# Folding the layer norm's scale of the first two row tiles into the exponential, moving the Q weights ahead of the fourth x tile, and writing a new order of the first stage

## The chip, the cores and the metric

One NeuronCore of a Trainium2 chip runs the whole program. The metric is the device time of one execution in microseconds (us). Before the change four runs gave a median of 213.01 us (212.72 to 213.26). The profile is one further execution of the same program; its own device time is 213.03 us, and the span from its first to its last instruction is 211.4 us.

## The reference

Shapes: x is 2048 rows of 512, `wqkv` 512x1536, `wo` 512x512, `w_gate` and `w_up` 512x1792, `w_down` 1792x512, all bf16. Attention has 32 heads of 16.

```python
xn = (x - mean(x)) / sqrt(var(x) + 1e-5)               # row by row
q, k, v = xn @ wqkv                                     # 32 heads of 16
phi = lambda t: where(t > 0, t + 1, exp(t)) + 1e-6
kv  = einsum("bhsd,bhse->bhde", phi(k), v);  z = sum over rows of phi(k)
o   = (phi(q) @ kv) / (phi(q) . z + 1e-6)
out = x + o @ wo + (silu(xn @ w_gate) * (xn @ w_up)) @ w_down
```

## The kernel before

**Engines.** Every operation is put into one list by `K.add` with the keys that it reads and writes (lines 40 to 67). Each engine runs its own operations strictly in the order of that list, and semaphore waits are made from the keys. TensorE (PE) does matmuls and transposes, VectorE (DVE) and ScalarE (ACT) read PSUM, GpSimd (POOL) works in SBUF only, and SyncE (SP) and ACT issue DMAs. A DMA that waits for its data holds up everything behind it on the engine that issues it.

**Stage 1** takes the 2048 rows in 16 tiles of 128. The order in which its steps stand in the list is written out by hand as a string of letters with a tile number (lines 352 to 361). The letters, by engine:

- DVE: `S` statistics of a row tile (L228 and L231); `L` normalise (L241); `V` a PSUM copy; `s` and `u` the last step of phi for k and for q (L316).
- ACT: `R` rstd = exp(-0.5 ln(var + eps)) (L235 and L237); `A` normalise with two per-row operands (L251); `E` a PSUM copy of a transposed tile (L276); `x` and `y` the exponential for k and q (L305).
- POOL: `N` the product mean*rstd that `A` needs (L246); `P` normalise (L256 and L259); `m` and `n` the clamp min(exp, 1 + 1e-6) (L309).
- PE: `T` four 128x128 transposes (L269); `k` and `q` a projection of one tile, four 128x512 matmuls (L297); `G` four matmuls that add xn^T phi(k) to four PSUM banks (L321); `F` filler matmuls.
- SP: `D`, a DMA transpose of a normalised tile into `xnT` (L284).

So phi is a chain over three engines: PE projection, ACT exp, POOL min, DVE max-and-add, which leaves `pk` or `pq` in SBUF. Projections take PSUM banks 4 to 7 in turn (`nextbank`), so a projection can't start until `s` or `u` has read the one four before it. Tiles 0 to 2 are transposed by PE (banks 0 to 2, copied out by ACT or DVE), tiles 3 to 15 by DMA. Instead of v and kv the kernel forms G = xn^T phi(k) (512x512, banks 0 to 3) and multiplies it by the V weights later.

Ahead of all that stand the table load, the loads (lines 185 to 196: x tile 0 in two halves, then x1, the K weights in two halves, x2, and the Q weights in two halves with x3 between them on SP's queue), some constants on POOL, and `NWARM` = 10 matmuls of 512 columns on constants (L218).

**Stage 2** starts with the loads of the other weights, issued by SP behind the last `D`. It runs 56 gate and up steps (`gu`, L384, in four chunks of 512 rows, Silu on ACT L392, product on DVE L397), the small matmuls that turn G into M = blockmask(kv) @ wo (L409, L457), the sum z of phi(k) (`z_add`: ten tiles on POOL, six on DVE), the division of phi(q) by its denominator (`pz_mul` on POOL, `divide` on DVE, a DMA transpose), and 16 output tiles (`ogroup`, L463 and L467) with the residual added by DVE (L473).

Of the kernel before, what the change touches and what calls it, by code (L numbers as in the profile page):

```python
# [9 lines left out]
P = 128  # L10
# [13 lines left out]
NWARM = 10  # L24
NFILL = 3
# [82 lines left out]
def bass_parallel_sum__linear_attn_block__swiglu_ffn__prompt_kernel(nc, A_x, A_wqkv, A_wo, B_x, B_w_gate, B_w_up, B_w_down, out):  # L108
# [5 lines left out]
    with contextlib.ExitStack() as es:  # L114
# [6 lines left out]
        xn = sb("xn", [P, NT, D], bf)  # L121
        xnT = sb("xnT", [P, NDC, S], bf)
# [28 lines left out]
        nm = sb("nm", [P, NT], f32)  # L151
        banks = [E(nc.psum_tensor("pb%d" % i, [P, 512], f32)) for i in range(8)]

        def B(i):
            return ("bank", i)
# [30 lines left out]
        for h, eng in ((0, "sp"), (1, "act")):  # L186
            load(eng, ("x", 0, h), x_sb[:, 0, h * 256:h * 256 + 256], xin[0:P, h * 256:h * 256 + 256])
        xload("sp", 1)
        wload("act", 1, 0, 2)
        wload("sp", 1, 1, 2)  # L190
        xload("act", 2)
        wload("act", 0, 0, 2)
        xload("sp", 3)
        wload("sp", 0, 1, 2)
        for t in range(4, 16):
            xload("sp", t)
# [27 lines left out]
        def xk(t):  # L224
            return [("x", t)] if t else [("x", 0, 0), ("x", 0, 1)]
# [7 lines left out]
        def rs(t):  # L233
            sl = slice(t, t + 1)
            K.add("act", lambda e: e.activation(lnv[:, sl], mv[:, t, 1:2], ACT.Ln, bias=eps5[:, :], scale=1.0),  # L235
                  r=[("mv", t), ("eps5",)], w=[("lnv", t)])
            K.add("act", lambda e: e.activation(rstd[:, sl], lnv[:, sl], ACT.Exp, scale=-0.5),  # L237
                  r=[("lnv", t)], w=[("rs", t)])

# [27 lines left out]
        def transp(t, b, lo=0, hi=NDC):  # L267
            tb = tview(b, hi - lo)
            K.add("pe", [(lambda e, c=c: e.transpose(tb[:, c - lo, :], xn[:, t, c * P:(c + 1) * P], ident[:, :]))  # L269
                         for c in range(lo, hi)], r=[("xn", t), ("ident",)], w=[B(b)])  # L270

        def evac(t, b, eng="act", lo=0, hi=NDC):
            src = tview(b, hi - lo)
            dst = xnT[:, lo:hi, t * P:(t + 1) * P]
            if eng == "act":
                K.add("act", lambda e: e.activation(dst, src, ACT.Copy), r=[B(b)], w=[("xnT", t, lo)])  # L276
            else:
                K.add("dve", lambda e: e.tensor_copy(dst, src), r=[B(b)], w=[("xnT", t, lo)])

        def xkeys(t):  # L280
            return [("xnT", t, 0), ("xnT", t, 2)] if t == 0 else [("xnT", t, 0)]

        def dmat(t):
            K.add("sp", lambda e: e.dma_start_transpose(out=xnT[:, :, t * P:(t + 1) * P], in_=xn[:, t, :]),  # L284
                  r=[("xn", t)], w=[("xnT", t, 0)], dma=True)
# [9 lines left out]
        def proj(col, i, t):  # L295
            b = nextbank()
            K.add("pe", [(lambda e, c=c: e.matmul(  # L297
                banks[b][:, :], xnT[:, c, t * P:(t + 1) * P], wqkv[:, c, col:col + D],
                start=(c == 0), stop=(c == NDC - 1))) for c in range(NDC)],
                r=xkeys(t) + [("wqkv", i, 0), ("wqkv", i, 1)], w=[B(b)])  # L300
            at[i, t] = b

        def phi_exp(i, t):
            b = at[i, t]
            K.add("act", lambda e: e.activation(ef[:, b - 4, :], banks[b][:, :], ACT.Exp), r=[B(b)], w=[("ef", b - 4)])  # L305

        def phi_min(i, t):
            buf, bkey = ef[:, at[i, t] - 4, :], ("ef", at[i, t] - 4)
            K.add("pool", lambda e: e.tensor_scalar(  # L309
                out=buf, in0=buf, scalar1=1.0 + 1e-6, scalar2=0.0, op0=ALU.min, op1=ALU.max),  # L310
                r=[bkey], w=[bkey])

        def phi_sum(i, t):
            b = at[i, t]
            dst, dkey = ((pk[:, t, :], ("pk", t)) if i else (pq[:, t, :], ("pq", t)))
            K.add("dve", lambda e: e.scalar_tensor_tensor(  # L316
                out=dst, in0=banks[b][:, :], scalar=1e-6, in1=ef[:, b - 4, :], op0=ALU.max, op1=ALU.add),
                r=[B(b), ("ef", b - 4)], w=[dkey])

        def gacc(t):  # L320
            K.add("pe", [(lambda e, c=c: e.matmul(  # L321
                banks[c][:, :], xn[:, t, c * P:(c + 1) * P], pk[:, t, :],
                start=(t == 0), stop=(t == NT - 1))) for c in range(NDC)],
                r=[("xn", t), ("pk", t)], w=[B(c) for c in range(NDC)])
# [4 lines left out]
        def z_add(half, i):  # L329
            acc, key = zacc[:, half, :], ("zacc", half)  # L330
            t = NZP * half + i
            first, fkey = (pk[:, t - 1, :], ("pk", t - 1)) if i == 1 else (acc, key)
            K.add("dve" if half else "pool",
                  lambda e: e.tensor_tensor(out=acc, in0=first, in1=pk[:, t, :], op=ALU.add),  # L334
                  r=[fkey, ("pk", t)], w=[key])

        def stat(t):
# [4 lines left out]
            "S": stat, "R": rs, "L": lna_dve, "P": lna_pool, "N": nmr, "A": lna_act, "T": lambda t: transp(t, t % 4),  # L342
            "E": lambda t: evac(t, t % 4), "V": lambda t: evac(t, t % 4, "dve"), "D": dmat,
            "k": lambda t: proj(D, 1, t), "x": lambda t: phi_exp(1, t), "m": lambda t: phi_min(1, t), "s": lambda t: phi_sum(1, t),
            "q": lambda t: proj(0, 0, t), "y": lambda t: phi_exp(0, t), "n": lambda t: phi_min(0, t), "u": lambda t: phi_sum(0, t), "G": gacc,
            "F": lambda t: keep_busy(t, 256)}

        def run(text):
# [4 lines left out]
            S0 R0 S1 L0 R1 L1 S2 T0 E0 F2 T1 V1 R2 L2 k0 k1 x0 m0 S3 T2 S4 x1 m1 E2 R4 s0 q1 R3 L4 k2 x2 N3 A3  # L353
            q2 s1 m2 y1 S5 R5 G0 D4 S6 s2 n1 G1 q0 y2 G2 D3 u1 R6 q4 N5 A5 S8 y0 k3 n2 N6 A6 u2 k4 y4 x3 n0 x4
            n4 m3 u0 m4 S13 D5 q3 R8 u4 s3 P8 D6 S7 k5 y3 R13 D8 n3 G3 s4 x5 k6 R7 S9 R9 N7 q6 G4 m5 A7 u3 s5
            S12 x6 q5 G5 N9 m6 S10 A9 y6 s6 y5 q8 R10 D7 k8 N13 n6 R12 u6 y8 G6 n5 x8 D9 u5 A13 k7 x7 S15 S11 k9
            P10 n8 u8 x9 R11 m8 D10 s8 m7 q9 m9 R15 P15 s7 y9 q7 G7 k10 D13 n9 L11 L12 s9 y7 q10 D11 G8 y10 n7
            n10 S14 G9 R14 x10 u7 u9 u10 k11 m10 N14 x11 s10 D15 q13 y13 A14 D12 m11 n13 s11 q11 y11 k12 D14 u13
            x12 m12 k13 k15 n11 x15 m15 u11 G10 x13 m13 s12 G11 q15 q14 y15 n15 s13 s15 k14 x14 m14 y14 q12 s14
            G12 y12 n12 n14 u15 G13 G14 u14 u12 G15  # L360
# [34 lines left out]
        def hop(j):  # L395
            C, fc = j // NFC, j % NFC
            K.add("dve", lambda e: e.tensor_tensor(  # L397
                out=hT[:, C % 2, fc, :], in0=banks[gb(j) + 1][:, :], in1=sil[:, j % 2, :], op=ALU.mult),
                r=[B(gb(j) + 1), ("sil", j % 2)], w=[("hT", C % 2, fc)])
# [37 lines left out]
        def divide(t):  # L437
# [3 lines left out]
                r=[("pz", i)], w=[("den", i)])  # L441
            K.add("dve", lambda e: e.tensor_scalar(
                out=den[:, i, :], in0=den[:, i, :], scalar1=1e-6, scalar2=None, op0=ALU.add),
                r=[("den", i)], w=[("den", i)])
# [121 lines left out]
```

## Time and profile before

| | |
|---|---|
| median of 4 runs | 213.01 us (212.72 to 213.26) |
| the profiled execution: device time | 213.03 us |
| the profiled execution: span | 211.4 us |
| PE busy | 208.1 us, 98% of the span |
| DVE / ACT / POOL busy | 125.4 / 69.8 / 55.7 us |
| first matmul on data (a transpose of x tile 0) | starts at 5.21 us |
| first projection | starts at 6.30 us |
| first matmul of stage 2 (L384) | starts at 48.48 us in the chain |
| last matmul ends, last output lands | 209.37 us, 211.36 us |

How to read it: all times inside the trace count from the first instruction of the span. A 512-column matmul is shown as 379 ns long, but the next one starts 216 ns after it, since matmuls are pipelined; a projection or a `G` of four matmuls therefore takes 0.863 us of PE's time. The device time is 1.65 us longer than the span.

### The profile page before, as it was taken

What the parts mean: (1) busy time and instruction counts of PE and PEld (TensorE: products, weight loads), DVE (VectorE), ACT (ScalarE), POOL (GpSimd) and SP (SyncE); (2) the same over time, 40 slices, a digit from 0 to 9 for tenths busy, and PEclk for the clock granted to TensorE, in tenths of its full rate; (3) what the DMA queues carried; (4) which work ended last, traced back from release to release, by engine and by line L of the source; (5) the groups of instructions that cost most, each with busy time, mean ns of one, the idle gap of its engine ahead of it and who ended that gap; (6) DMA issues with size and microseconds to landing.
All of it is one profiled execution on the core that took longest, in us unless ns stands there. A gap on an engine that the chain in (4) does not pass through costs nothing.

```text
span 211.4 us, 2659 instructions
## 1 busy us (share of the span) xinstructions
PE 208.1 (98%) x991; PEld 95.7 (45%) x991; DVE 125.4 (59%) x217; ACT 69.8 (33%) x138; POOL 55.7 (26%) x81
## 2 busy tenths in 40 slices
PE   7999999999999999999999999999999999999996
PEld 2444444444544444444444444444444444444455
DVE  3899985546874888564654765473649453532121
ACT  4697974546364332122131313121123122130000
POOL 3267664559913222220210220120204000000000
PEclk9999999999999999999999999999999999999999
DMA  6942333499910021103101011101011101100101
GB/s 183 357 115 49 72 63 62 119 380 372 353 43 0 8 45 25 50 0 53 25 25 45 4 29 50 25 25 50 19 34 25 50 16 38 25 25 9 40 25 53
DMA packets 26765, 15.78 MB, mean 75 GB/s; under 512 B 16512, under 2 KB 26752, under 8 KB 26752
## 3 DMA queue, kind: packets, MB, share of 16 engines
q1 hardware_dynamic: 25920, 14.88, 25.2%
q10 hardware_dynamic: 832, 0.72, 1.1%
q8 instruction: 8, 0.13, 0.3%
q14 instruction: 5, 0.04, 0.1%
HBM read 9.70 MB, written 2.10 MB: 56 GB/s over the span
## 4 chain that ended last, share of the span: by engine, by line
PE 96%; DVE 1%; DMA 1%; ACT 0%; issue 0%
PE pb L384 46%; PE pb L467 23%; PE pb L297 13%; PE pb L463 7%; PE pb L321 7%; DMA x_sb<-in_A_x_dram 1%; DVE stats L228 1%; PE pb L409 0%; PE pb L457 0%; PE pb L269 0%; DVE out_sb L473 0%; DVE xn L241 0%; DVE mv L231 0%; ACT lnv L235 0%; PE pb L425 0%; ACT rstd L237 0%
## 5 line engine op out<-in xcount | busy, mean ns | idle before, releaser
L392 ACT ACTIVATE sil<-pb 128x512 bf16<-128x512 f32 x56 | 33.3, 597 | 101.2 <-PE pb L384 98.8
L397 DVE TENSOR_TENSOR hT<-pb,sil 128x512 bf16<-128x512 f32 x56 | 38.0, 687 | 36.2 <-PE pb L384 33.4
L384 PE MATMUL pb<-xnT,wu 128*128 128x512 bf16 x224 | 57.8, 379 | 0.0
L384 PE MATMUL pb<-xnT,wg 128*128 128x512 bf16 x224 | 57.8, 379 | 0.0
L467 PE MATMUL pb<-wd,hT 128*128 128x512 bf16 (+1 forms) x238 | 51.2, 366 | 0.0
L434 POOL TENSOR_TENSOR pz<-pq,zbc 128x512 f32<-128x512 bf16 x16 | 18.5, 1162 | 86.0 <-DVE den L439 78.5
L467 PEld LDWEIGHTS pb<-wd,hT 128*128 128x128 bf16 x238 | 23.3, 98 | 25.1
L384 PEld LDWEIGHTS pb<-xnT,wu 128*128 128x128 bf16 x224 | 21.9, 98 | 26.0
L384 PEld LDWEIGHTS pb<-xnT,wg 128*128 128x128 bf16 x224 | 21.9, 98 | 25.9
L473 DVE TENSOR_TENSOR out_sb<-pb,x_sb 128x512 bf16<-128x512 f32 (+1 forms) x17 | 11.2, 661 | 33.5 <-PE pb L467 33.5
L297 PE MATMUL pb<-wqkv,xnT 128*128 128x512 bf16 x128 | 29.6, 379 | 0.0
L309 POOL TENSOR_SCALAR ef<-ef 128x512 bf16<-128x512 bf16 x32 | 19.5, 614 | 18.5 <-ACT ef L305 18.3
L305 ACT ACTIVATE ef<-pb 128x512 bf16<-128x512 f32 x32 | 18.3, 590 | 9.1 <-PE pb L297 8.8
L297 PEld LDWEIGHTS pb<-wqkv,xnT 128*128 128x128 bf16 x128 | 12.1, 98 | 15.4 <-ACT xnT L276 0.4
L446 DVE TENSOR_TENSOR pq<-pq,rden 128x512 bf16<-128x512 bf16 x16 | 17.5, 1092 | 0.6
L463 PE MATMUL pb<-M,pk 128*128 128x512 bf16 (+1 forms) x68 | 16.6, 366 | 0.0
L321 PE MATMUL pb<-pk,xn 128*128 128x512 bf16 x64 | 15.4, 379 | 0.0
L316 DVE SCALAR_TENSOR_TENSOR pk<-pb,ef 128x512 bf16<-128x512 f32 x16 | 10.8, 679 | 4.9 <-POOL ef L309 4.9
L228 DVE BATCH_NORM_STATS2 stats<-x_sb 128x6 f32<-128x512 bf16 x16 | 10.9, 680 | 3.3 <-DMA x_sb<-in_A_x_dram 3.2
L316 DVE SCALAR_TENSOR_TENSOR pq<-pb,ef 128x512 bf16<-128x512 f32 x16 | 10.7, 682 | 3.6 <-POOL ef L309 3.5
L439 DVE TENSOR_REDUCE den<-pz 128x32 f32<-128x512 f32 x16 | 10.8, 675 | 0.0
L334 POOL TENSOR_TENSOR zacc<-zacc,pk 128x512 f32<-128x512 f32 x8 | 10.3, 1292 | 0.6
(46 smaller groups left out, 76.9 us busy)
## 6 DMA issues: line engine op xcount, KB each, us to landing
out_dram<-out_sb SPq DMA_DIRECT2D x15, 128.0 KB, 1.7
x_sb<-in_A_x_dram SPq DMA_DIRECT2D x14, 128.0 KB, 5.0
wg<-in_B_w_gate_dram SPq DMA_DIRECT2D x2, 896.0 KB, 7.7
wu<-in_B_w_up_dram SPq DMA_DIRECT2D x2, 896.0 KB, 10.0
wd<-in_B_w_down_dram SPq DMA_DIRECT2D x2, 896.0 KB, 14.2
wqkv<-in_A_wqkv_dram ACTq DMA_DIRECT2D x2, 256.0 KB, 4.6
wqkv<-in_A_wqkv_dram SPq DMA_DIRECT2D x2, 256.0 KB, 5.0
wqkv<-in_A_wqkv_dram SPq DMA_DIRECT2D x1, 512.0 KB, 7.8
```

What stands on the lines that cost most here:

```text
L297: K.add("pe", [(lambda e, c=c: e.matmul(banks[b][:, :], xnT[:, c, t * P:(t + 1) * P], wqkv[:, c, col:col + D], start=(c == 0), stop=(c == ...
L305: K.add("act", lambda e: e.activation(ef[:, b - 4, :], banks[b][:, :], ACT.Exp), r=[B(b)], w=[("ef", b - 4)])
L309: K.add("pool", lambda e: e.tensor_scalar(out=buf, in0=buf, scalar1=1.0 + 1e-6, scalar2=0.0, op0=ALU.min, op1=ALU.max), r=[bkey], w=[bkey])
L316: K.add("dve", lambda e: e.scalar_tensor_tensor(out=dst, in0=banks[b][:, :], scalar=1e-6, in1=ef[:, b - 4, :], op0=ALU.max, op1=ALU.add), ...
L321: K.add("pe", [(lambda e, c=c: e.matmul(banks[c][:, :], xn[:, t, c * P:(c + 1) * P], pk[:, t, :], start=(t == 0), stop=(t == NT - 1))) for ...
L384: fns.append(lambda e, c=c, b=b, w_=w_: e.matmul(banks[b][:, :], w_[:, c, fc * P:(fc + 1) * P], xnT[:, c, C * 512:(C + 1) * 512], start=(c ...
L392: K.add("act", lambda e: e.activation(sil[:, j % 2, :], banks[gb(j)][:, :], ACT.Silu), r=[B(gb(j))], w=[("sil", j % 2)])
L397: K.add("dve", lambda e: e.tensor_tensor(out=hT[:, C % 2, fc, :], in0=banks[gb(j) + 1][:, :], in1=sil[:, j % 2, :], op=ALU.mult), r=[B(gb( ...
L434: K.add("pool", lambda e: e.tensor_tensor(out=pz[:, t % 2, :], in0=pq[:, t, :], in1=zbc[:, :], op=ALU.mult), r=[("pq", t), ("zbc",)], w=[( ...
L446: K.add("dve", lambda e: e.tensor_tensor(out=heads(pq[:, t, :]), in0=heads(pq[:, t, :]), in1=rden[:, i, :][:, :, None].broadcast_to([P, NH ...
L463: fns = [(lambda e, g=g: e.matmul(banks[bank][:, 0:hi - lo], pk[:, t, g * P:(g + 1) * P], M[:, g, lo:hi], start=(g == 0), stop=False)) for ...
L467: fns = [(lambda e, fc=fc: e.matmul(banks[bank][:, 0:hi - lo], hT[:, C % 2, fc, jj * P:(jj + 1) * P], wd[:, fc, lo:hi], start=False, stop= ...
```

## The change

Parts, as they stand in the code:

1. **Tiles 0 and 1 are only centred** ahead of their projections. Their transposed copies (`xcT`) hold x - mean, so a projection gives std times the wanted value. The exponential puts that right with two per-row operands, `scale=rstd` and `bias=ln(std)`; its result is std*exp(t). The clamp and the floor are scaled as well (`cap` = std*(1 + 1e-6), `flo` = std*1e-6), so `pk` and `pq` of these two tiles are std*phi. In G the other factor is `xg` = (x - mean)*rstd^2; in the sum z the rows are multiplied by rstd; in the division `pq` scales numerator and denominator alike, and the 1e-6 becomes `flo`.
2. Tile 0 is centred, transposed (two 128x128 transposes each, banks 0 and 1) and copied out in two halves. For tile 1 the mean comes from ACT (`M`: a Copy with an accumulated sum), without waiting for the statistics. Normalised copies of tiles 0 and 1 are still made (`P0` on POOL, `L1` on DVE) and go to `xnT` by two more DMA transposes (`D0`, `D1`) for stage 2; 15 in all, where there were 13. Tile 2 is transposed by PE as before (`X`, `Y`).
3. **Loads**: the Q weights' first half moves from ACT's queue to SP's, ahead of x3; the second half moves from SP's queue, behind x3, to ACT's. The K weights and x0 to x2 keep their places.
4. A projection's four matmuls are two groups of two, and each waits for its own half of the weights (and, for tiles 0 and 1, of the transposed tile).
5. `NWARM` goes from 10 to 8, and the filler `F2` is gone.
6. **The order string is new.** It holds the same 32 projections and 16 `G` groups, but starts k0 k1 q1 q0 k2 q2 G1 G0 G2, has only four `G` among the next 26 projections, and ends with nine `G` in a row. Normalising is done by POOL for 8 tiles (3 before), by ACT for 5 (7) and by DVE for 2 and the centred ones (6).
7. Scratch copies of tiles 0 and 1 lie in parts of `hT` and `pz` that are used later.

The diff, cut to its core:

```diff
-NWARM = 10
-NFILL = 3
+CENTRED = (0, 1)
+NWARM = 8
...
+        xhalf("sp", 0, 0)
+        xhalf("act", 0, 1)
         xload("sp", 1)
-        wload("act", 1, 0, 2)
-        wload("sp", 1, 1, 2)
+        wpart("act", 1, 0)
+        wpart("sp", 1, 1)
         xload("act", 2)
-        wload("act", 0, 0, 2)
-        xload("sp", 3)
-        wload("sp", 0, 1, 2)
-        for t in range(4, 16):
+        wpart("sp", 0, 0)
+        wpart("act", 0, 1)
+        for t in range(3, 16):
             xload("sp", t)
...
+        def powers(t):
+            sl = slice(t, t + 1)
+            K.add("act", lambda e: e.activation(std[:, sl], lnv[:, sl], ACT.Exp, scale=0.5), r=[("lnv", t)], w=[("std", t)])
+            K.add("act", lambda e: e.activation(r2[:, sl], lnv[:, sl], ACT.Exp, scale=-1.0), r=[("lnv", t)], w=[("r2", t)])
+            K.add("act", lambda e: e.activation(lstd[:, sl], lnv[:, sl], ACT.Copy, scale=0.5), r=[("lnv", t)], w=[("lstd", t)])
...
+        def neg_mean(t):
+            K.add("act", lambda e: e.activation(
+                junk, x_sb[:, t, :], ACT.Copy, scale=-1.0 / D, accum_out=negm[:, t:t + 1]),
+                r=xk(t), w=[("negm", t), ("junk",)])
+
+        def centre_half(t, h):
+            K.add("dve", lambda e: e.tensor_scalar(
+                out=xc[:, t, h * H:(h + 1) * H], in0=x_sb[:, t, h * H:(h + 1) * H], scalar1=mv[:, t, 0:1], scalar2=None,
+                op0=ALU.subtract), r=xk(t) + [("mv", t)], w=[("xc", t, h)])
...
         def proj(col, i, t):
             b = nextbank()
-            K.add("pe", [(lambda e, c=c: e.matmul(
-                banks[b][:, :], xnT[:, c, t * P:(t + 1) * P], wqkv[:, c, col:col + D],
-                start=(c == 0), stop=(c == NDC - 1))) for c in range(NDC)],
-                r=xkeys(t) + [("wqkv", i, 0), ("wqkv", i, 1)], w=[B(b)])
+            src = xcT if t in CENTRED else xnT
+            for h in (0, 1):
+                K.add("pe", [(lambda e, c=c: e.matmul(
+                    banks[b][:, :], src[:, c, t * P:(t + 1) * P], wqkv[:, c, col:col + D],
+                    start=(c == 0), stop=(c == NDC - 1))) for c in (2 * h, 2 * h + 1)],
+                    r=([("xcT", t, h)] if t in CENTRED else xkeys(t)) + [("wqkv", i, h)], w=[B(b)])
             at[i, t] = b
 
         def phi_exp(i, t):
             b = at[i, t]
+            if t in CENTRED:
+                K.add("act", lambda e: e.activation(ef[:, b - 4, :], banks[b][:, :], ACT.Exp, bias=lstd[:, t:t + 1], scale=rstd[:, t:t + 1]),
+                      r=[B(b), ("rs", t), ("lstd", t)], w=[("ef", b - 4)])
+                return
...
         run("""
-            S0 R0 S1 L0 R1 L1 S2 T0 E0 F2 T1 V1 R2 L2 k0 k1 x0 m0 S3 T2 S4 x1 m1 E2 R4 s0 q1 R3 L4 k2 x2 N3 A3
...
+            S0 M1 b0 a0 d0 R0 c0 C1 S1 e0 P0 W1 h0 r0 k0 w1 R1 o0 S2 J0 r1 k1 x0 j1 R2 q1 m0 x1 L2 o1 s0 X2 y1
+            q0 m1 S5 D0 Y2 n1 s1 k2 R5 S8 P5 q2 x2 S9 R8 D5 m2 G1 y2 P8 s2 R9 G0 u1 y0 N9 D8 G2 S10 n0 A9 n2
+            k5 u0 R10 D9 u2 P10 q5 x5 S12 m5 q8 D10 y5 s5 R12 n5 k8 y8 S6 P12 k9 x8 u5 n8 R6 D12 G5 S11 x9 m8
+            q9 u8 R11 N6 m9 A6 s8 q10 P11 s9 y9 D6 k10 S4 y10 n9 k12 n10 D11 u9 x10 R4 S7 m10 G8 x12 N4 u10 R7
+            q6 m12 A4 s10 P7 q12 s12 y6 D4 S14 n6 q11 y12 u6 D7 R14 n12 k6 y11 N14 u12 k11 n11 x6 S15 A14 m6
+            k4 u11 R15 D14 G12 s6 x11 P15 x4 S13 q7 m11 D15 R13 q4 m4 s11 y7 N13 s4 k7 n7 A13 u7 y4 q14 D13 x7
+            S3 n4 k14 y14 m7 u4 R3 G10 n14 s7 x14 L3 q15 m14 u14 D3 s14 q13 y15 L1 n15 k13 D1 y13 u15 n13 k15
+            x13 u13 m13 k3 x15 s13 m15 q3 x3 s15 m3 G4 y3 s3 n3 G7 u3 G14 G3 G15 G6 G11 G9 G13
         """)
```

The letters that are new in it: `M` the negative mean on ACT; `b`, `a` and `C` centring on DVE; `c`, `d`, `W`, `X` transposes on PE; `e`, `h`, `Y` PSUM copies on ACT and `w` one on DVE; `r` three per-row powers on ACT; `o` cap and floor on POOL; `J` (POOL) and `j` (DVE) the tiles `xg`.

## Prediction

> **What bounds the kernel now.** I read the page first (busy shares), then the chain of work that ended last, then the timeline of the first 14 us.
>
> ```profile
> PE 208.1 (98%) x991; PEld 95.7 (45%) x991; DVE 125.4 (59%) x217; ACT 69.8 (33%) x138; POOL 55.7 (26%) x81
> ...
> PE 96%; DVE 1%; DMA 1%; ACT 0%; issue 0%
> ```
>
> PE sets the end. The only question is how much of the span PE spends before its useful work runs without gaps. The chain in order of time says where that begins:
>
> ```profile
> 0.83 2.30 DMA x_sb<-in_A_x_dram
> ...
> 5.93 0.40 PE pb L269 x4
> 6.32 1.89 PE pb L297 x8
> 8.21 0.22 PE pb L269 x4
> 8.44 2.92 PE pb L297 x12
> 11.36 1.73 PE pb L321 x8
> ```
>
> From 5.93 us on the chain never leaves PE until the last output. But twelve matmuls in 2.92 us are not gapless: from the `G` stage on, four take 0.863 us (8 in 1.73), so twelve should take 2.59. The weight loads in the timeline show the three waits of `q1`, `k2` and `q2`:
>
> ```profile
> 8.42 0.55 PEld L297 LDWEIGHTS pb<-wqkv,xnT 128*128 128x128 bf16 x4 [0.16 <-DMA wqkv<-in_A_wqkv_dram]
> ...
> 9.38 0.55 PEld L297 LDWEIGHTS pb<-wqkv,xnT 128*128 128x128 bf16 x4 [0.42 <-ACT xnT L276]
> ...
> 10.32 0.55 PEld L297 LDWEIGHTS pb<-wqkv,xnT 128*128 128x128 bf16 x4 [0.39 <-DVE pk L316]
> ```
>
> From the single matmul starts, PE really stands still 0.15, 0.09 and 0.06 us there. After 11.19 us (first matmul of `G0`) nothing is lost any more. So all that the new order can win lies before that point: the useful matmuls are the same in number. What it can lose lies anywhere.
>
> **A yardstick.** Ahead of `G0` at 11.19 stand five projections and the transposes of tile 2. The new order has four projections (k0 k1 q1 q0) and tile 2's transposes ahead of `k2`. One projection is 0.863, so the old kernel's level at that amount of work is 11.19 - 0.86 = 10.33 us. If the new `k2` starts at 10.33 and no gap follows, the time is unchanged; each 0.1 earlier is 0.1 us won.
>
> **What the Trainium skill says.** (1) "ScalarE: Activation LUTs", section What ACT_TABLE_LOAD costs: each per-row operand adds about 93 ns to an ACTIVATE. The trace agrees: one-column Ln with a bias operand 287 ns, Exp with immediates 203; the 512-wide `A` with two operands 802, the plain copy 594. (2) "DMA: Bandwidth & Descriptors", section Issuing engines are not separate DMA queues: DMAs of SP and ACT interleave on the same 16 engines. The trace agrees: x2 (ACT) and the K weights' second half (SP) land together, at 5.88 and 6.07. So swapping queues gives no bandwidth; only bytes taken out of the way count. (3) "TensorE: Matmul & The Clock Gate", Part 1: PE runs at half rate until it was busy for about 3.4 us, in free-running windows. Here warm-up matmuls start 427 ns apart until about 4.3 us, the full clock is recorded from 4.34, 3.50 us after the first one.
>
> **The change, step by step.** Rows used for durations (mean ns):
>
> ```profile
> L316 DVE SCALAR_TENSOR_TENSOR pk<-pb,ef 128x512 bf16<-128x512 f32 x16 | 10.8, 679 | 4.9 <-POOL ef L309 4.9
> L305 ACT ACTIVATE ef<-pb 128x512 bf16<-128x512 f32 x32 | 18.3, 590 | 9.1 <-PE pb L297 8.8
> L309 POOL TENSOR_SCALAR ef<-ef 128x512 bf16<-128x512 bf16 x32 | 19.5, 614 | 18.5 <-ACT ef L305 18.3
> L251 ACT ACTIVATE xn<-x_sb,nm,rstd 128x512 bf16<-128x512 bf16 x7 | 5.6, 802 | 0.0
> L276 ACT ACTIVATE xnT<-pb 128x512 bf16<-128x512 bf16 x2 | 1.2, 594 | 0.2 <-PE pb L269 0.2
> L259 POOL TENSOR_SCALAR xn<-x_sb,nm,rstd 128x512 bf16<-128x512 bf16 x3 | 2.3, 780 | 0.3
> ```
>
> Handovers, from single starts and ends: PE to ACT 0.04, ACT to POOL 0.085, POOL to DVE 0.035, DVE or ACT to PE 0.055. Independent neighbours overlap by 0.08 (DVE) to 0.095 (ACT). A projection is readable 1.06 us after it starts (0.65 to its last matmul, 0.38 for that, 0.04).
>
> *Tile 0, centring instead of normalising.* Statistics end at 4.07 as before. Then two half subtractions on DVE. The trace has no 256-column one; the 512-column `L` takes 0.38 to 0.41 and an operation on 2 columns 0.18, so each is between 0.18 and 0.41; I take 0.32. Transposes at 4.49 and 4.72, ACT copies them out in 0.38 each (594 ns less 256 of 512 columns at 0.83 ns), ready at 5.43 and 5.71. `k0`'s first pair can start at 5.49 (before: 6.30). Its second pair waits for the K weights' second half, which lands at 6.07 and isn't moved: 6.11. So `k0` is done at 6.55 and `k1` at 7.41 on PE. Before: 8.05. Tile 1's ACT mean (between 0.59, the plain copy, and 0.80 or somewhat more; I take 0.65) and `w1` (0.39, ends 6.08) are in time for `k1`. This wins 0.64 us, if what follows is ready.
>
> *The Q weights.* It isn't. `q1` now stands directly behind `k1` and wants to start at 7.41. The landing records of before have the Q halves at 8.05 and 8.38, and x3 at 7.20. Taking x3's 128 KB out of their way saves 8 KB on each DMA engine; x4 lands 0.37 after the last Q half, so that is worth 0.35. Both halves now run side by side and end together, near 8.38 - 0.35 = 8.03. `q1` starts at about 8.05: 0.37 earlier than before's 8.42, but tile 2's transposes (0.22) still lie behind it.
>
> *From `q1` to `k2`.* ACT's queue holds, in order, x0, R2, x1, y1, Y2 (tile 2's copy, which `k2` needs). With two per-row operands x0, x1 and y1 take 0.77 (590 plus twice 0.09; bounds 0.59 and 0.80). x0 runs 6.75 to 7.52, R2 to 7.95, x1 to 8.64: in time. y1 must await `q1`: 8.05 + 1.06 = 9.11, to 9.88. Y2 is queued behind it though tile 2 has been transposed by 9.30: 9.79 to 10.38. `k2` starts at 10.44, while PE is free from `q0` at 10.00. Against the yardstick: 10.44 - 10.33 = +0.11 us. **The earlier start is eaten by the Q weights and then by the copy of tile 2 behind a lengthened exponential.** The other feeders of `k2` and `q2` are earlier: s0 ends 8.98, s1 10.62.
>
> *Middle of stage 1.* Before, 11 of 28 bank reuses had only three or four PE groups between; now 24 have, 8 of them three. The chain exp, min, max-and-add with handovers takes 0.20 + 0.59 + 0.085 + 0.614 + 0.035 + 0.68 + 0.055 = 2.26 us against 3 x 0.863 = 2.59. I walked DVE, ACT and POOL down the new order from `k2` to `L1` with the rows above: a statistics pair costs DVE 0.80, a max-and-add 0.60, POOL's normalising 1.05. DVE is then full: between S12 at 16.0 and the end of s14 at 36.9 it has 9 x 0.80 + 20 x 0.60 + 0.33 = 19.5 us of work in 20.9. Every reuse still has its bank free before PE comes, by 0.15 us (`u8` ahead of `q10`) to 0.8. The DMA transposes (2.45 us from issue to landing) arrive 0.2 us (D8) or more ahead of their projections. I take zero here; bounds zero (there is no gap to win) and about 0.6.
>
> *Into stage 2.* `D1` is last on SP and holds the loads of `w_gate` and `w_up`. L1 follows s14, so `D1` issues near 37.3 and the loads near 38.5; before 38.99. `w_up`'s first half landed 46.5 there, 2.8 us before its first use. Nothing is lost. The two longer first steps of z (some 1.6 us of POOL) lie where POOL starts about 4 us earlier than before; z is not awaited until after 59 us. `flo` in the division, the hazards on `hT`, and the finer waits cost nothing: their producers ended tens of us before. Fewer warm-up matmuls (two of 0.43) and no filler remove nothing from the path: PE waits for x there.
>
> Sum: 213.03 + 0.11 = 213.1 us. That run stands 0.02 from the median of before, so no correction.
>
> **The rivals.**
>
> *The Q weights come in one piece early (212.6 us).* In the trace 15 of 16 DMA engines had landed the Q halves by 6.96 and 7.70; one engine, behind since x3 (6.39 against 7.20), held both up to 8.05 and 8.38. If it isn't late, Q lands near 7.35, `q1` starts at 7.41, then L2 (8.40) sets tile 2's transposes, y1 ends 9.32, Y2 9.82, `k2` starts 9.88: 0.45 under the yardstick. Before hardly gains from that, since `k2` there waits for ACT. For: nothing in the trace names a cause of the late engine. Against: it stayed 0.8 late through every later load of x.
>
> *PE's clock comes a window later (213.5 us).* Eight warm-up matmuls keep PE busy to 0.84 + 8 x 0.427 = 4.26, the grant came at 4.34, and behind it now come 1.2 us with little but transposes. If the grant slips by one period, to 4.34 + 3.50 = 7.84, `k0` and `k1` run at 0.427 a matmul and `q1` starts at 8.38: `k2` at 10.77, +0.44. It decides as soon as the grant falls later than about 7.2. Against: the busy stretch nearly fills one period.
>
> *The vector queue falls behind (213.6 us).* DVE at 19.5 of 20.9 us has 0.15 us to spare at `u8`; beyond that each 0.1 of lateness is 0.1 us of PE, and I price 0.5. Against: before, DVE worked 9.35 of the 10 us from 16 to 26 and PE lost nothing, though with wider bank spacing.
>
> *The change doesn't act:* covered by the first case, 213.0 to 213.1.
>
> **Chances.** 213.1 as worked out (own range 212.8 to 213.4): 0.48. Q early: 0.22. Late clock: 0.12. Vector queue: 0.18. The measurement can tell 0.2% from no change, which is 212.58 and 213.44. Q early straddles the lower bound, the two slow rivals mostly lie above the upper: faster 0.17, same 0.54, slower 0.29. The range 212.5 to 213.8 takes in Q early and most of both slow ones.
>
> **What would show it.** Right: first projection near 5.5, its second pair near 6.1, `q1` waiting for a DMA until about 8, `k2` waiting for the ACT copy until 10.4, no PE wait after. Wrong: `q1` near 7.4 (Q early); matmuls 427 ns apart after 5.5 (clock); PE waits on DVE lines between 15 and 42 us (vector queue), or on a DMA transpose.

## The result, and the profile after

| | before | after |
|---|---|---|
| median, runs side by side | 213.18 us (212.60 to 214.25, 48 runs) | 214.63 us (213.55 to 217.11, 29 runs) |
| profiled execution: device time | 213.03 us | 213.81 us |
| profiled execution: span | 211.4 us | 212.4 us |

The ratio is 1.0067, with a 95% interval of 1.0054 to 1.0080: slower by 0.67%, where 213.1 (212.5 to 213.8) was forecast. The profiled execution is one of the quick ones of its kernel, 0.82 us under the median, so the two traces explain 1.0 us of span and not the whole difference of the medians. One of the 29 runs after (217.11 us) and one of the six of e11 below (217.05) lie over 1.5% above the quickest of their kernel and count as slow ones, which the ratios leave out.

The page of the kernel after, busy times and shares of the chain that ended last:

```profile
PE 208.4 (98%) x987; PEld 95.1 (45%) x987; DVE 127.0 (60%) x218; ACT 70.9 (33%) x145; POOL 62.5 (29%) x97
...
PE 93%; DVE 2%; ACT 2%; DMA 1%; issue 1%; SPq 0%; DVEq 0%
```

PE still sets the end, but its share of the chain fell from 96% to 93%: the chain now leaves PE. The start of the chain does not show where; there this trace is ahead of before. The chain of the kernel after, in order of time (start, length, what):

```profile
8.62 0.40 PE pb L347 x4
9.02 0.86 PE pb L378 x4
9.88 0.02 issue
9.90 1.90 PE pb L378 x8
11.81 2.59 PE pb L413 x12
```

The first `G` matmul starts at 11.64 us, behind six projections; before it was at 11.19 behind five. One projection is 0.86, so 12.06 would be level, and the new start is **0.42 us ahead**. The twelve `G` matmuls in 2.59 us are gapless; before, the twelve ahead of the first `G` took 2.92. What PE's weight loads waited for in the whole span of the kernel after (us in total, times, longest):

```profile
PEld pb L492 <- DVE hT L505: 1.7, 2, 1.1
PEld pb L378 <- DVE pq L403: 1.0, 2, 0.5
...
PEld pb L378 <- DMA wqkv<-in_A_wqkv_dram: 0.7, 2, 0.4
...
PEld pb L378 <- ACT xnT L355: 0.5, 1, 0.5
```

The last two rows are the waits of the start that before has too. The first two are new. They are waits of the weight loads, which run ahead of the matmuls, so I took the loss from the starts of single matmuls, 0.216 us apart when nothing is late. After the start four intervals are longer: 14.880 to 15.253 (0.16 lost), 27.997 to 28.413 (0.20), 73.333 to 73.840 (0.29) and 77.088 to 78.027 (0.72). With the start, -0.42 + 0.16 + 0.20 + 0.29 + 0.72 = +0.95 us, against +1.0 in the span. The last two, **1.01 us, lie in stage 2**, at a place that the change hardly touches. The chain there:

```profile
65.94 6.92 PE pb L492 x32
72.86 0.03 issue
72.89 0.02 DVEq L100
72.91 0.19 issue
73.10 1.28 DVE hT L505 x2
74.38 0.60 DVE den L547
74.99 0.03 issue
75.01 1.25 DVE den L551
76.27 0.02 issue
76.29 0.36 DVE rden L554
...
77.29 0.69 DVE hT L505
77.98 0.05 issue
78.03 6.22 PE pb L492 x28
```

From 73.1 to 78.0 the chain runs over DVE: the product `hT` that frees the gate and up banks stands behind the division, and in the division stands `L551`, the floor add on 32 columns, for 1.25 us. The timeline of the kernel after around the first such division:

```profile
70.11 0.68 DVE L547 TENSOR_REDUCE den<-pz 128x32 f32<-128x512 f32 x1
...
70.82 1.25 DVE L551 TENSOR_SCALAR den<-den,flo 128x32 f32<-128x32 f32 x1
70.86 1.17 POOL L542 TENSOR_TENSOR pz<-pq,zbc 128x512 f32<-128x512 bf16 x1 [1.93 <-DVE den L547]
...
72.10 0.35 DVE L554 RECIPROCAL rden<-den 128x32 f32<-128x32 f32 x1
...
72.49 0.69 DVE L555 TENSOR_TENSOR pq<-pq,rden 128x512 bf16<-128x512 bf16 x1
```

And of the kernel before, DVE and POOL at the same place:

```profile
70.16 0.68 DVE L439 TENSOR_REDUCE den<-pz 128x32 f32<-128x512 f32 x1
...
70.87 0.18 DVE L442 TENSOR_SCALAR den<-den 128x32 f32<-128x32 f32 x1
70.92 1.16 POOL L434 TENSOR_TENSOR pz<-pq,zbc 128x512 f32<-128x512 bf16 x1 [1.93 <-DVE den L439]
...
71.09 0.35 DVE L445 RECIPROCAL rden<-den 128x32 f32<-128x32 f32 x1
71.48 1.15 DVE L446 TENSOR_TENSOR pq<-pq,rden 128x512 bf16<-128x512 bf16 x1
```

The only difference in the code of the division is that `scalar1` is the per-row `flo` for tiles 0 and 1 in place of 1e-6. The add ends 0.04 us after POOL's product `pz` (70.86 to 72.03). Before, POOL's product also starts 0.05 us after the add, the add takes 0.18, and it is DVE's own product that overlaps POOL's and takes 1.15, where 0.69 is its length alone (the last two divisions before, with no POOL product beside them). So the division takes 3.07 us from the start of the reduction to the end of the product, where it took 2.47. The groups of the kernel after by shape point to the operand (that it isn't the place is for e1 to show):

```profile
L551 DVE TENSOR_SCALAR den<-den 128x32 f32<-128x32 f32 x14 | 2.5, 182 | 0.5
L551 DVE TENSOR_SCALAR den<-den,flo 128x32 f32<-128x32 f32 x2 | 2.5, 1245 | 0.1
```

### The profile page after: what moved, and what is told of

Read it like the earlier page. It is cut to its first block, busy times and chain, and to the rows that moved or that the text cites. A ratio compares the mean times of both kernels' runs of the same rounds, so it can differ in the third digit from the quotient of the medians.

```text
span 212.4 us, 2690 instructions
## 1 busy us (share of the span) xinstructions
PE 208.4 (98%) x987; PEld 95.1 (45%) x987; DVE 127.0 (60%) x218; ACT 70.9 (33%) x145; POOL 62.5 (29%) x97
## 4 chain that ended last, share of the span: by engine, by line
PE 93%; DVE 2%; ACT 2%; DMA 1%; issue 1%; SPq 0%; DVEq 0%
PE pb L492 44%; PE pb L576 23%; PE pb L378 12%; PE pb L572 7%; PE pb L413 7%; DMA x_sb<-in_A_x_dram 1%; DVE hT L505 1%; DVE den L551 1%; PE pb L517 0%; PE pb L566 0%; ACT ef L387 0%; ACT lnv L259 0%; ACT rstd L261 0%; DVE den L547 0%; DVE xn L317 0%
## 5 line engine op out<-in xcount | busy, mean ns | idle before, releaser
L378 PE MATMUL pb<-wqkv,xnT 128*128 128x512 bf16 x112 | 25.5, 379 | 0.1
L395 POOL TENSOR_SCALAR ef<-ef 128x512 bf16<-128x512 bf16 x28 | 17.1, 615 | 5.0 <-ACT ef L390 4.5
L390 ACT ACTIVATE ef<-pb 128x512 bf16<-128x512 f32 x28 | 16.4, 591 | 4.8 <-PE pb L378 4.5
L378 PEld LDWEIGHTS pb<-wqkv,xnT 128*128 128x128 bf16 x112 | 10.7, 98 | 14.0 <-DVE pq L403 1.0
L555 DVE TENSOR_TENSOR pq<-pq,rden 128x512 bf16<-128x512 bf16 x16 | 16.6, 1035 | 0.6
L413 PE MATMUL pb<-pk,xn 128*128 128x512 bf16 x56 | 13.1, 379 | 0.0
L403 DVE SCALAR_TENSOR_TENSOR pq<-pb,ef 128x512 bf16<-128x512 f32 x14 | 9.5, 678 | 1.7 <-POOL ef L395 1.6
L572 PEld LDWEIGHTS pb<-M,pk 128*128 128x128 bf16 x68 | 6.7, 98 | 7.4
L403 DVE SCALAR_TENSOR_TENSOR pk<-pb,ef 128x512 bf16<-128x512 f32 x14 | 9.4, 686 | 0.7 <-POOL ef L395 0.7
```

What stands on the lines that cost most here:

```text
L378: K.add("pe", [(lambda e, c=c: e.matmul(banks[b][:, :], src[:, c, t * P:(t + 1) * P], wqkv[:, c, col:col + D], start=(c == 0), stop=(c == ...
L395: K.add("pool", lambda e: e.tensor_scalar(out=buf, in0=buf, scalar1=top, scalar2=0.0, op0=ALU.min, op1=ALU.max), r=[bkey] + tkeys, w=[bkey])
L403: K.add("dve", lambda e: e.scalar_tensor_tensor(out=dst, in0=banks[b][:, :], scalar=low, in1=ef[:, b - 4, :], op0=ALU.max, op1=ALU.add), r ...
L413: K.add("pe", [(lambda e, c=c: e.matmul(banks[c][:, :], src[:, t, c * P:(c + 1) * P], pk[:, t, :], start=first, stop=last)) for c in range ...
L555: K.add("dve", lambda e: e.tensor_tensor(out=heads(pq[:, t, :]), in0=heads(pq[:, t, :]), in1=rden[:, i, :][:, :, None].broadcast_to([P, NH ...
L572: fns = [(lambda e, g=g: e.matmul(banks[bank][:, 0:hi - lo], pk[:, t, g * P:(g + 1) * P], M[:, g, lo:hi], start=(g == 0), stop=False)) for ...
```

## The experiments

**What was to be told apart.** Theory: the per-row floor lets POOL's product take the SBUF ports that DVE and POOL share, the add then waits for the whole product, and both waits of PE follow from that. The Trainium skill, "SBUF — State Buffer", section Who interferes with whom, says that these ports go to one of the two engines for a whole instruction, and that the one that issues first has them. The first half agrees with the 1.25 us that end with POOL's product; the second doesn't quite, since the add is recorded 0.04 us ahead of the product and yet loses. Rival one: PE's full clock comes too late, because there are 8 warm-up matmuls for 10. Rival two: the per-row form itself is slow, POOL or not. Rival three: the new load order. Rival four: the middle of stage 1, where the DMA transposes land shortly before they are used.

| kernel | median (runs) | ratio to before, 95% interval |
|---|---|---|
| e1 constant floor | 213.17 (22) | 1.0007 [0.9990, 1.0024] |
| e2 ten warm-up matmuls | 214.65 (9) | 1.0067 [1.0045, 1.0089] |
| e3 old kernel, eight and no filler | 214.48 (22) | 1.0048 [1.0028, 1.0068] |
| e4 old kernel, per-row floor | 214.37 (10) | 1.0051 [1.0032, 1.0070] |
| e5 POOL's product waits | 213.70 (22) | 1.0024 [1.0011, 1.0037] |
| e6 old kernel, new load order | 213.48 (14) | 1.0009 [0.9998, 1.0021] |
| e7 e1, old load order | 213.57 (14) | 1.0011 [0.9995, 1.0026] |
| e8 e1, ten warm-up matmuls | 213.41 (14) | 1.0014 [1.0000, 1.0028] |
| e9 e1, three `G` moved up | 212.95 (22) | 0.9989 [0.9977, 1.0000] |
| e10 e9, `Y2` ahead of `y1` | 213.12 (22) | 0.9991 [0.9981, 1.0001] |
| e11 e1, four warm-up matmuls | 214.66 (6) | 1.0086 [1.0048, 1.0124] |
| e12 e9, per-row floor on ACT | 212.96 (13) | 0.9987 [0.9972, 1.0002] |

The kernel before, run beside them on the same chips, had medians of 213.21 to 213.38.

### e1: the floor a constant again

```diff
-            eps, ekeys = (flo[:, t:t + 1], [("flo", t)]) if t in CENTRED else (1e-6, [])
+            eps, ekeys = 1e-6, []
```

> The changed kernel with the floor of the two first divisions as the constant 1e-6 again instead of std*1e-6 per row (this changes the denominator of 256 rows by less than 1e-6). Theory 1 (the per-row operand makes DVE's two small adds 1.25 us long instead of 0.18, and PE pays for it at 73 and 77 us): both adds 0.18 us, no PE gap between 70 and 80 us, span about 1.0 us shorter than the changed kernel's, median near 213.6. Rival (the gaps at 73 and 77 come from something else in stage 2, such as the earlier start of the z sums): PE gaps of 0.3 and 0.7 us stay and the time stays near 214.6.

213.17 us, 1.46 below the kernel after and level with the one before: with this one operand the whole loss is gone. That is more than the 1.0 us expected; but by the ratios it is 1.3 us, and my estimate from their two intervals is 0.8 to 1.7, so the 1.0 of the trace is inside. In its trace all 16 adds take 0.18 us, at the same places, and PE has no gap near 73 or 77 us. Its first `G` starts at 12.13 us, level with before and not ahead of it as in the trace of the kernel after. A gap of 0.30 us at 22.4 us, before a projection whose transpose came late, is still there.

### e2 and e3: the warm-up alone

Ten matmuls in the kernel after; and in the kernel before, eight and no `F2`:

```diff
-NWARM = 8
+NWARM = 10
```

> The changed kernel with ten warm-up matmuls instead of eight. Clock theory (with eight the full clock is granted late, at 5.8 us in the profile and later in other runs, so that the runs spread from 213.6 to 217.1 and the median is 0.8 above the profiled run): spread of the runs back to about 1 us and median lower by about 0.5, near 214.1, although the first transposes start 0.5 us later. Rival (the warm-up has nothing to do with the spread): spread unchanged, median unchanged or up to 0.5 higher through the later transposes.

> The kernel before with eight warm-up matmuls and without the two fillers, nothing else. Clock theory: the full clock comes later than 4.3 us in most runs, median 0.3 to 1.0 above 213.2 and a wider spread, some runs above 214.3. Rival (warm-up irrelevant): within 0.1 of 213.2 with the same spread.

In the kernel after, two more warm-up matmuls bring nothing: 214.65 us, and the two waits in stage 2 are still there (74.17 to 74.67, 77.92 to 78.84; 0.28 and 0.71 lost). So the clock isn't the cause of the loss. This trace lies at the median of the kernel after. What it has beyond the trace of the kernel after is a later start: the Q halves landed at 7.89 and 8.71 us (there 7.46 and 7.89), and the first `G` starts at 12.46, 0.82 later. In the **old** kernel the shorter warm-up does cost: 214.48 us, in two clusters, 212.89 to 213.47 (6 runs) and 214.05 to 215.55 (16). My sentence that fewer warm-up matmuls and no filler remove nothing from the path was not safe for that kernel. The one trace fell in the lower cluster (213.46), so what the upper cluster waits for isn't shown.

### e4: only the floor's operand, in the kernel before

```diff
-                out=den[:, i, :], in0=den[:, i, :], scalar1=1e-6, scalar2=None, op0=ALU.add),
+                out=den[:, i, :], in0=den[:, i, :], scalar1=eps, scalar2=None, op0=ALU.add),
```

with `eps` a 128x1 tile that holds 1e-6 for tiles 0 and 1, and the constant for the others.

> The kernel before with the floor of the divisions of tiles 0 and 1 read from a one-column tile that holds 1e-6, nothing else. Theory 1: the two adds take about 1.25 us, PE gaps of about 0.3 and 0.7 us near 73 and 77 us, median about 1.0 above 213.2, near 214.2. Rival (the operand is harmless, the new order of stage 1 causes the gaps): both adds 0.18 us, 213.2.

The same number in every row, only read from SBUF: +1.1 us, and both waits of PE (73.622 to 74.121, 77.368 to 78.301: 0.28 and 0.72 lost). Nothing else of the change is in this kernel. DVE and POOL in its timeline:

```profile
71.11 1.24 DVE L445 TENSOR_SCALAR den<-den,flo 128x32 f32<-128x32 f32 x1
71.15 1.16 POOL L436 TENSOR_TENSOR pz<-pq,zbc 128x512 f32<-128x512 bf16 x1 [1.94 <-DVE den L441]
```

### e5: the per-row floor, with POOL held back until it is done

```diff
-                  r=[("pq", t), ("zbc",)], w=[("pz", t % 2)])
+                  r=[("pq", t), ("zbc",)] + ([("den", t % 2)] if t in (2, 3) else []), w=[("pz", t % 2)])
```

> The changed kernel, per-row floor kept, but the POOL products of tiles 2 and 3 wait until the floor add of the buffer's former tile has been done. Lock theory (the add with a per-row operand loses the race for the SBUF ports that DVE and POOL share to the POOL product that starts 0.04 us after it, and stands still until that ends): both adds near 0.2 us, the product pq*rden 1.15 us again, no PE gaps at 73 and 77 us, time near that of the constant floor, 213.2. Rival (a 32-column add with a per-row operand is that slow by itself): adds stay at 1.25 us, PE gaps stay or grow, 214.6 or more.

The extra key makes POOL's products of tiles 2 and 3 wait for the adds of tiles 0 and 1. The timeline of that kernel:

```profile
71.28 0.24 DVE L551 TENSOR_SCALAR den<-den,flo 128x32 f32<-128x32 f32 x1
...
71.60 1.16 POOL L542 TENSOR_TENSOR pz<-pq,zbc 128x512 f32<-128x512 bf16 x1 [2.21 <-DVE den L551]
...
71.94 1.37 DVE L555 TENSOR_TENSOR pq<-pq,rden 128x512 bf16<-128x512 bf16 x1
```

Both per-row adds take 0.24 us when POOL isn't running: 0.06 more than with a constant, not 1.07. Rival two falls. The time goes from 214.63 to 213.70, not to the 213.2 expected: POOL starts later, DVE's product of the same division takes 1.37 where 1.15 was expected, the division takes 2.74 us, and one wait of 0.36 us at 77.2 stays. DVE's product ends 0.55 us after POOL's here (73.31 and 72.76), and 0.55 after it in the kernel before (72.63 and 72.08), though it started 0.34 us into POOL's product here and 0.56 there. That is what standing still until POOL has ended gives; if the two merely slowed each other, the earlier start would have brought an earlier end. The trace also has PE wait for a DMA transpose in stage 1 (0.64 us by the starts of single matmuls):

```profile
22.83 1.02 PE L378 MATMUL pb<-wqkv,xnT 128*128 128x512 bf16 x4 [0.48 <-DMA xnT<-xn]
```

### e6 and e7: the load order alone, and all but it

e6 puts the new order into the kernel before; e7 puts the old one back into e1.

```diff
-        wload("act", 0, 0, 2)
-        xload("sp", 3)
-        wload("sp", 0, 1, 2)
-        for t in range(4, 16):
+        wload("sp", 0, 0, 2)
+        wload("act", 0, 1, 2)
+        for t in range(3, 16):
```

> The kernel before with the new order of loads alone (Q halves side by side, ahead of x3). The prediction's step: Q lands 0.35 to 0.9 earlier, but the second k projection waits for the ACT copy of tile 2, so the first G starts at most 0.1 earlier: 213.1 to 213.2, no change. Rival (the Q weights were what held the start): first G 0.3 or more earlier, 212.9 or less.

> The changed kernel with the constant floor and with the loads of the kernel before (Q halves behind and beside x3). If the earlier Q weights are what the new start rests on, q1 waits until 8.4 as before and the first G starts 0.4 to 0.9 later than in the changed kernel (11.64): 213.6 to 213.9. Rival (the copy of tile 2 or the clock sets the start anyway): within 0.2 of the constant-floor kernel, 213.2.

In the old kernel the order is worth nothing (213.48, 1.0009), as the prediction says; in its trace `k2` waits for ACT's copy again (0.58 us, to 10.00). In the new one the old order's median is 0.40 higher than e1's, but the two intervals lie over each other, so by the times the gain of the new order isn't settled. e7's trace had the Q halves at 8.86 and 9.18 us, PE 1.62 us idle ahead of `q1`, and its first `G` at 13.04. The traces of all runs say what the new start rests on: in eight of the nine with the order q1, X2, y1, Y2 the first `G` starts 3.75 to 3.97 us after the second Q half has landed (7.71 to 9.18), in the ninth (e9, full clock only at 6.60 us) 4.37 after it. Level with before would be a landing near 8.2.

### e8 and e11: how long a warm-up the new start needs

The diff is e1's, with `NWARM` 10 and 4.

> The changed kernel with the constant floor and ten warm-up matmuls. Clock theory: fewer runs above 214 than with eight (there 6 of 22), median within 0.3 of 213.2, since the later first transposes and the earlier full clock nearly cancel. Rival (the slow runs of the new order have another cause): the same share of runs above 214, median 0.2 to 0.4 higher.

> The changed kernel with the constant floor and only four warm-up matmuls. Clock theory: the full clock is granted well after 6 us, the first projections run 427 ns a matmul, first G later than 12.1 us by 0.5 or more, median 0.4 or more above 213.2. Rival (the clock's delay hides behind the Q weights): within 0.2 of 213.2.

Ten bring nothing: 213.41, and 3 of 14 runs lie above 214 us, where e1 has 5 of 22 (not 6, as the expectation says). That is about the same share, so it is the rival that fits: nothing ties the long runs of the new order to the eight warm-up matmuls. Four cost 1.3 us against e1 (214.43 is the median of the five runs in the ratio). The grant of the full clock came at 7.98 us in e11's trace, where it was 5.83 in that of the kernel after, and the first projections run at half rate. PE's timeline of e11:

```profile
5.33 0.61 PE L347 MATMUL pb<-ident,hT 128*128 128x128 bf16 x4 [0.34 <-DVE hT L294]
5.73 4.06 PE L378 MATMUL pb<-wqkv,hT 128*128 128x512 bf16 x12
```

Twelve matmuls take 4.06 us; the same twelve took 2.91 in the kernel after, from 5.63. But only the first six start 0.427 us apart. `q1`, the last four, then waits for the Q halves, which landed at 8.58 and 9.14 in this trace, so it could not have ended earlier at full clock either. In this trace, the quickest of the six, the late clock hides behind the Q weights. That it costs the 1.3 us in the others is likely, since the warm-up is all that differs from e1, but no trace of them shows it. The clock isn't what made the change slower. e8's trace shows the other loss, a transpose that made PE lose 0.87 us by the starts of single matmuls:

```profile
29.98 1.02 PE L378 MATMUL pb<-wqkv,xnT 128*128 128x512 bf16 x4 [0.71 <-DMA xnT<-xn]
```

### e9 and e10: more time between the transposes and their projections

e9 is e1 with `G9`, `G10` and `G6` taken from the end of the order and put ahead of `k12`, `q11` and `q4`; e10 also lets ACT copy tile 2 out ahead of `y1`.

```diff
-            ... S4 y10 n9 k12 n10 ...  S14 n6 q11 y12 ...  R13 q4 m4 ...
+            ... S4 y10 n9 G9 k12 n10 ...  S14 n6 G10 q11 y12 ...  R13 G6 q4 m4 ...
```

> The changed kernel with the constant floor and with three G groups (tiles 9, 10, 6) moved forward, ahead of the projections k12, q11 and q4; same work. Spare theory (in the new order a DMA transpose lands only 0.2 to 1 us ahead of its projection, so each transpose that takes 3.6 us instead of 2.4 leaves PE idle): the spare of tiles 12, 11, 4 and 7 grows by 0.9 to 1.7 us, no PE gap over 0.1 us between 16 and 42 us in the profile, median 0.2 to 0.5 below the constant-floor kernel, 212.7 to 213.0. Rival (vector engines set the gaps): gaps of 0.3 us or more on DVE waits stay, time unchanged at 213.2; or the weights of stage 2, issued about 2.6 us later, make PE wait near 49 us and it is slower.

> As the last one, with ACT's copy of tile 2 ahead of the exponential of q1. The prediction's step (k2 waits for a copy that stands behind that exponential): k2 starts 0.2 us earlier when the Q weights are early and up to 0.7 earlier when they are late, median 0.1 to 0.4 below the last one. Rival (k2 is then held by something else, or u1 becomes late): no difference.

e9 gives 212.95 us, and after 15.5 us its trace has no long interval between two matmuls at all. Its interval ends at 1.0000, so it is level with the kernel before or a little under it. Against e1 it is 0.22 lower; that fits rival four as a smaller second loss, but the intervals overlap. The long runs say more: with a constant floor and the order as in the change (e1, e7, e8) 11 of 50 runs lie above 214 us, with the three `G` moved up (e9, e10, e12) 2 of 57, and the kernel before, run beside them, has 7 of 163. So the tight transposes show in the long runs rather than in the median; which transposes were late in those runs wasn't profiled. e10 moves the waits and gains nothing: `k2` no longer waits for the copy, and `q2`, `G2` and the projection behind it wait for DVE in its place (10.635 to 11.000, 13.385 to 13.760 and 14.418 to 14.976).

### e12: the floor as the change has it, but added by ScalarE

```diff
+            if t in CENTRED:
+                K.add("act", lambda e: e.activation(den[:, i, :], den[:, i, :], ACT.Identity, bias=flo[:, t:t + 1], scale=1.0),
+                      r=[("den", i), ("flo", t)], w=[("den", i)])
```

on top of e9, in place of the add on DVE for tiles 0 and 1.

> The kernel with three G steps spread out, but with the floor of tiles 0 and 1 per row again, added by ScalarE (Identity with one per-row operand) in place of VectorE. It computes the reference with its own floor. If the loss in stage 2 is the wait for the SBUF ports that VectorE and GpSimd share, an add on ScalarE doesn't meet it: reduction 0.68, two handovers of 0.04, the add about 0.31 (a one-column Ln with a bias operand takes 0.29, and 31 more columns), reciprocal 0.35, product 1.15, so 2.57 us for a division where the constant has 2.39 and the per-row add on VectorE 2.99. The wait of PE near 73 us goes, near 77 at most 0.3 stays: 213.0 to 213.3 us, level with the kernel before or a little under. If any longer division costs as the per-row add did, or the add holds up the Silu behind it on ScalarE, both waits of PE stay: 213.9 us.

The timeline of e12 at the first division:

```profile
69.92 0.67 DVE L547 TENSOR_REDUCE den<-pz 128x32 f32<-128x512 f32 x1
...
70.63 0.32 ACT L551 ACTIVATE den<-den,flo 128x32 f32<-128x32 f32 x1 [1.65 <-DVE den L547]
70.67 1.16 POOL L542 TENSOR_TENSOR pz<-pq,zbc 128x512 f32<-128x512 bf16 x1 [1.93 <-DVE den L547]
...
70.98 0.35 DVE L557 RECIPROCAL rden<-den 128x32 f32<-128x32 f32 x1 [0.39 <-ACT den L551]
71.37 1.01 DVE L558 TENSOR_TENSOR pq<-pq,rden 128x512 bf16<-128x512 bf16 x1
```

ACT's add starts the same 0.04 us ahead of POOL's product and takes 0.32 us. The detour over two engines costs nothing in the end: 2.46 us from the start of the reduction to the end of the product, where before had 2.47 and after 3.07. DVE's product starts 0.70 us into POOL's and again ends 0.55 after it (72.38 and 71.83), so as long as the steps ahead of it end within POOL's product, their length doesn't count. PE has no gap in stage 2. 212.96 us is level with e9's 212.95, which has the constant, and 1.67 under the change as it was made; against the kernel before it can't be told from no change, though the whole interval but 0.0002 lies on the quick side.

## Why the prediction was wrong, point by point

**The failed step** is in *Into stage 2*: "`flo` in the division, the hazards on `hT`, and the finer waits cost nothing: their producers ended tens of us before." That looked only at when the operand is ready. It is ready: no wait for it appears. What changed is the form of the instruction that reads it, and the sentence leaves its duration at the 0.18 us of `L442`, which has a constant. The trace of before had no per-row add of 32 columns, so it had to be bounded from both sides, and the upper bound stood in that trace: POOL's product starts 0.05 us behind the add, lasts 1.16, and slows the DVE product beside it from 0.69 to 1.15. That step measures +1.01 us of PE, not 0: the add takes 1.25 us, and the `hT` product behind it frees PE's bank late, twice. In medians e1 gives 1.46, e4 1.1, and e12 (with the `G` moved up as well) 1.67.

**Tile 0's centring and the yardstick**: right. `k0` started at 5.63 us (forecast 5.49), the half copies took 0.37 each (0.38), and the exponential with two per-row operands takes 0.77 us, as worked out. The level itself hangs on one trace: e4, whose start is the old one, has its first `G` at 11.43, not 11.19.

**The Q weights and `q1` to `k2`**: the mechanism right, two sizes off. `q1` did wait for its DMA, but the halves landed at 7.46 and 7.89 and not together at 8.03, and `Y2`, behind `y1` on ACT as forecast, started at 9.26 and not 9.79. `k2` began at 9.90, as in the rival "Q early" (9.88), and in this trace the start won 0.42 us where the forecast had lost 0.11. This landing varies from run to run: 7.37 and 7.57 in e9's trace, 8.86 and 9.18 in e7's with the old loads. Where it came near the forecast, in e1's trace (8.17), the first `G` started at 12.13; the forecast's `k2` at 10.44 puts it at 12.17. So the path was right, and which side of level a single run falls on is the luck of the landing.

**The middle of stage 1**: taken at zero with a bound of 0.6; 0.36 us in this trace, within the bound. Of it 0.16 is `q5` waiting for a DVE step, the cause I had priced. The other 0.20 ahead of `k4` is the one I had waved through: the transpose of tile 4 landed at 28.28 us, 3.2 us after its issue. (The view of waits names DVE there too, but that step had ended at 27.84.) At its usual length it would have had 0.7 us to spare, and the late ones of e1, e5 and e8 0.7 to 1.05; single ones take 0.7 to 1.7 us longer, which cost 0.64 us in e5's trace and 0.87 in e8's. The trace of before had one of 3.17 us, so the price could have been read there; the least spare in its order was 0.96.

**The warm-up**: nothing lost in the new kernel, as forecast (e2, e8), but the reason given, that PE waits for x there, doesn't carry: in the old kernel the same cut cost 1.2 us (e3, 214.48 against 213.24 beside it).

**The rivals**: for the start it came out as "Q early" had it; none of them is what made the kernel slower. I priced the DVE queue in the wrong stage, between 16 and 37 us where its load is highest. The page of before has DVE busy 8 tenths from 69 to 84 us too, and there a late DVE step goes straight to PE, since `hT` frees the banks of a later gate and up step.

**What stays open**: the gaps in the trace are 1.01 us, the operand is worth 1.1 to 1.5 in the medians; the intervals don't tell these apart. That the median of the kernel after lies 0.82 us above its trace is likely the start: e2's trace, at that median, has the same two waits and a start 0.82 later behind later Q weights. But e2 has ten warm-up matmuls, and of the kernel after itself there is only the one trace. Why a per-row add stands behind an instruction that starts 0.04 us after it isn't seen, nor whether the constant add gets the ports in time or doesn't need them. That it stands still until POOL has ended, and that the operand and POOL's product are both needed for it, rests on e1, e4, e5 and e12.

## What to carry to other kernels

A constant that becomes a per-row operand is a new instruction, not the old one with another number: look at what runs beside it on the engine that can hold it up (for DVE here, POOL), and if there is something, bound its time by the length of that neighbour. Then ask who stands behind it on its engine: 1.07 us more, twice, on 32 columns cost more than the 0.42 us that the whole rewriting of the start won in its best trace. Where the neighbour can't be moved, give the small step to an engine that it doesn't hold up (ACT, 0.32 us in e12). In a tight order, count a DMA transpose at its longest landing, not at its usual one.

## What the runs showed of the hardware that I had not expected

- A DVE add on 32 columns that starts 0.04 us **ahead of** a POOL product waits for its whole length if its scalar is read per row (1.24 to 1.25 us), and doesn't if it is a constant (0.18). Alone, the per-row add takes 0.24. Normalising steps of 512 columns with per-row scalars whose POOL neighbour starts 0.15 to 0.32 us behind them aren't held up (0.40 to 0.41, with or without it; 30.05 us before, 35.12 after, 35.78 and 37.30 in e1).
- Two kinds of DVE step, where they start inside a POOL step, end a fixed time after POOL's end, whenever they started: DVE's product in the division 0.54 to 0.55 us after it (started 0.34, 0.56 and 0.70 us in), the per-row steps `L304` and `L317` at the start of the kernel after 0.15 (0.84 and 0.54 us long beside POOL steps of 0.77 and 0.71, where a per-row normalising step took 0.38 to 0.41 before).
- A DMA transpose lands 2.4 to 2.7 us after its issue, but one or two in each trace take 2.8 to 4.2, and in the new order the first one, `D0`, issued near 9 us while x is still being loaded, 3.7 to 5.1. Most of the others that I compared lie over a fetch of 16 KB of instructions (about 1.0 us, at 25.8 us in the kernel after), but not all: the one of 3.17 at 30.16 us before doesn't. That the fetch is the cause was not tried.
- The full clock is recorded from 3.84 to 7.98 us over the traces that show it. For a kernel with eight or ten warm-up matmuls it varied from 3.84 to 6.60, so one trace doesn't tell where it falls; the Trainium skill, "TensorE: Matmul & The Clock Gate", Part 1, calls its windows free-running, which fits.
